# Banded attention with a gated MLP: an own PSUM tile for each MLP accumulator, two attention regions in the first batch, and a new planned order

## The chip, the cores and the metric

The kernel runs on one core of a Trainium2 chip. The metric is device time in microseconds (us), the median of several executions. Lower is better.

## The reference, cut to what matters

```python
# attention: q, k, v are (8 batches, 8 heads, 576 positions, 64)
scores = (q @ k^T) / 8
# heads 0-3: position i sees i-31..i; heads 4-7: every 32nd position up to i
attn = softmax(where(mask, scores, -1e9))          # exp(x - max) / (sum + 1e-9)
x = (attn @ v), heads side by side                  # (8, 576, 512)
# gated MLP: w_in (512, 1024), conv_w (3, 1024), w_out (1024, 512)
h = maximum(x @ w_in, 0)
c = conv_w[0]*h[s-1] + conv_w[1]*h[s] + conv_w[2]*h[s+1]
out = (h * sigmoid(c)) @ w_out
```

The MLP weights come as 64-bit floats.

## The kernel before, in words

**Attention.** Heads go in pairs, four pairs to a batch; a pair is called an attention unit here, numbered n over the whole run. Both masks are turned into a band: the strided heads are permuted so that each of 32 residues is a short local band. For each unit PE computes the scores (36 small matmuls, L459) into a PSUM region `psR[reg]`; VectorE takes the maximum and subtracts it (L470, L471), ScalarE the exponential (L473), VectorE the sum and reciprocal (L474, L476), and GpSimd normalises (L479). The result is transposed into `pt` in one of two ways: *turned* on PE (L439, with ScalarE copies L441), or by 32x32 transposes on VectorE (L482, L502) with ScalarE copies (L499). PE then multiplies by v into the same region (values, L508), and ScalarE and VectorE move it out as a high part `xh` (L522) and a low part `xl` (L523). q, k and v have two buffers (`slot`, n % 2).

**MLP.** Each float32 product is made of three passes over parts of reduced precision: high x high, low x high, high x low. The first product (`mm1`, L545) makes for each of 8 units f of 128 features two groups (halves of 288 positions) of 12 matmuls: four row blocks c times three passes. ScalarE evicts each group with a relu (L551) into one of three `h` buffers; then the convolution: ScalarE scales (L557), VectorE adds two weighted, shifted terms (L563, the "sums"), ScalarE takes the sigmoid (L566), VectorE multiplies (L568, the "gate"), ScalarE rounds to the high part `gh` (L414), and VectorE or GpSimd subtracts for the low part `gl` (L417; SPLIT_G says where). The second product (`mm2`, L585) makes 4 x 2 groups of 24 matmuls, evicted by ScalarE (L591) and written out by DMA (L592).

**Weights.** During the first batch, 8 + 8 weight tiles are loaded as 64-bit words and split into parts by ScalarE and VectorE (`from_f64`), with two matmuls on PE (L393, L394), and, where SPLIT_W says "a", a subtraction of the high part on PE (L400) so that ScalarE can do the last copy (L402) instead of VectorE (L404).

**PSUM.** There are four tiles of 1024 words a partition, r0 to r3. Attention uses the first 576 columns; later batches alternate r0 and r1, and the first batch's four units use r0, r1, r2, r0 (`region`). The four MLP accumulators are halves of r2 and r3:

```python
psR = [psum.tile([P, 1024], F32, name=f"r{i}") for i in range(4)]
psM = [psR[2 + i // 2][:, i % 2 * 512:i % 2 * 512 + 512] for i in range(NPM)]
```

MLP groups take the accumulators in turn (`state["m"] % NPM`), and so do the splits of the second weights; the splits of the first weights use only the two halves of r3.

**Order.** Nothing is written in the order in which it runs. `op` notes each step with an engine, an estimated duration, a due time and the buffers that it reads and writes; there ("M", 0) to ("M", 3) are four separate things. `Plan.order` runs a small model of the engines and emits the steps by their begin times in it. The due times are the table of numbers at the top. Each engine then executes its list strictly in order; the framework that allocates the tiles adds the waits between engines. All loads and stores go through one DMA queue, SP's.

Of the kernel before, what the change touches and what calls it, by code (L numbers as in the profile page):

```python
# [9 lines left out]
F32 = _mybir.dt.float32  # L10
F32R = _mybir.dt.float32r
BF16 = _mybir.dt.bfloat16
I32 = _mybir.dt.int32
# [6 lines left out]
P = 128  # L20
W = 32
# [7 lines left out]
PE_PENALTY = 1  # L29
RATE = 205.0  # L30

EYE_AT = -15.59
CONV_AT = 13.95
FIRST = "w0 k0 q0 v0 k1 w1 q2 q1 v1 k2 c0 w2 w3 q3 k3 v3 v2 w4"
WARM = 4
WARM_SCORES = [0, 0, 2, 4]
WARM_VALUES = [2, 2, 0, 0]
FIRST_AT = [18.9, -9.9, -37.3, -11.6]
SECOND_AT = [45.6, 109.8, 118.7, 107.8]
LATER_AT = [35.8, 46.3, 68.6, 52.7]  # L40
START = 27.38
START2 = 106.92
PERIOD = 46.51
MM1_STEP = 4.82
MM2_AT = 52.57
MM2_STEP = 31.88
LOAD_Q = 76.19
LOAD_V = 12.98
W_IN_AT = [43.1, 1.3, -17.1, 33.6, 22.0, 62.6, 49.8, 27.1]
W_OUT_AT = [55.4, 88.5, 74.3, 73.5, 54.9, 59.3, 84.9, 103.2]  # L50
SPLIT_W = "aavvvaaaaaaaavvv"
SPLIT_G = "vvvpvpvv"
FIRST_SPLIT_G = "vvvvvpvv"
TURNED = 2
FIRST_GATE = "vvvvvvvv"
FIRST_SCALE = "aaaaavaa"


class Plan:
# [184 lines left out]
def tile_banded_attention_gated_mlp(ctx, tc, qT, kT, vw, w_in, conv, w_out, mask, ident, eyes_in, out):  # L244
    nc = tc.nc
    B, NHP, D, _, S = qT.shape
# [7 lines left out]
    V, A, G, T, Q = "dve", "act", "pool", "pe", "dma"  # L254
    plan = Plan()
    op = plan.op
# [32 lines left out]
    cs = [misc[:, c0 + S * i:c0 + S * i + S] for i in range(NHB)]  # L289
    os_ = [misc[:, c0 + S * (NHB + i):c0 + S * (NHB + i) + S] for i in range(2)]  # L290
    psum = ctx.enter_context(tc.tile_pool(name="psum", bufs=1, space=PSUM))
    psR = [psum.tile([P, 1024], F32, name=f"r{i}") for i in range(4)]
    psM = [psR[2 + i // 2][:, i % 2 * 512:i % 2 * 512 + 512] for i in range(NPM)]
    NWS, NWA, NWT, NWL = 3, 2, 2, 1
    words = [const.tile([P, 4 * P, 2], I32, name=f"ws{i}") for i in range(NWS)]
    wa = [const.tile([P, 4 * P], I32, name=f"wa{i}") for i in range(NWA)]
# [5 lines left out]

    def slot(n):
        return n % NB

    def region(n):
        return (0, 1, 2, 0)[n] if n < NHP else n % 2

    def load_q(n, at):
        i, b, hp = slot(n), n // NHP, HPS[n % NHP]  # L310
# [8 lines left out]
    def load_v(n, at):  # L319
        i, b, hp = slot(n), n // NHP, HPS[n % NHP]  # L320
        v = buffers[i][2]
        op(Q, 260, at, lambda: nc.sync.dma_start(out=v, in_=vw[b, hp]), (), [("v", i)])

    def set_up(i, at):
        q, k, v, pt, t = buffers[i][:5]
# [40 lines left out]
    state = dict(m=0, h=0, last=None)  # L366
    seen = set()

    def convert(hi, lo, src, at, key, dat=None):
        c = nw[0]  # L370
        nw[0] += 1
        j, k = c % NWA, c % NWT
        if key[0] == "wi" and c < 3:
            i, ws = ("in", c), misc[:, 1024 * c:1024 * c + 1024].bitcast(I32).rearrange("p (n w) -> p n w", w=2)
        else:
            i, ws = c % NWS, words[c % NWS]
        op(Q, 400, at if dat is None else dat, lambda: nc.sync.dma_start(out=ws.rearrange("p n w -> p (n w)"), in_=src.bitcast(I32)), (), [("W", i)])
        t, tail = wt[k].bitcast(F32), wl[c % NWL]
        kt, kl = ("WT", k), ("WL", c % NWL)
        from_f64(ws[:, :, 1], ws[:, :, 0], wa[j], wt[k], tail, at, ("W", i), ("WA", j), kt, kl, False)  # L380

        def parts(x):
            return x.rearrange("p (c n) -> p c n", c=4)
        if key[0] == "wi":
            mi = 2 + c % 2
        else:
            mi = state["m"] % NPM
            state["m"] += 1
        ps = psM[mi]
# [6 lines left out]
        op(T, 1.1, at, whole, [kt, kl, "unit", "eyer"], [("M", mi)], table=4)  # L396
        if last:
            def rest():
                for x in range(4):
                    nc.tensor.matmul(ps[:, P * x:P * x + P], negr, hi()[:, x, :], start=False, stop=x == 3)  # L400
            op(T, 0.3, at, rest, [(key, "h"), "negr"], [("M", mi)])
            op(A, 0.59, at, lambda: nc.scalar.copy(lo(), parts(ps)), [("M", mi)], [(key, "l")])  # L402
        else:
            op(V, 0.69, at, lambda: nc.vector.tensor_tensor(out=lo(), in0=parts(ps), in1=hi().bitcast(F32), op=ALU.subtract),  # L404
               [("M", mi), (key, "h")], [(key, "l")])
# [25 lines left out]
    def turn(n, ps, ks, u0, n_u, key, at):  # L431
        i = slot(n)
        pt = buffers[i][3]

        def turns():
            for u in range(n_u):
                for e in range(2):
                    o = ps[0:96, 128 * u:128 * u + 128].rearrange("p (h x) -> p h x", h=2)[:, :, 32 * e:32 * e + 32]
                    nc.tensor.matmul(o, pad[:, u0 + u, 32 - 32 * e:128 - 32 * e], unit[:, e, :], start=True, stop=True)  # L439
        op(T, 0.112 * 2 * n_u, at, turns, ["tt", "unit"], [ks], table=3)  # L440
        op(A, 0.25 + 0.105 * n_u, at + 0.5, lambda: nc.scalar.copy(  # L441
            pt[:, :, u0:u0 + n_u, :].rearrange("p h u c -> p u h c"),
            ps[0:96, 0:128 * n_u].rearrange("p (u h c) -> p u h c", h=2, c=64)), [ks], [key])

    def attention(n, at, spread):
        i, hp = slot(n), HPS[n % NHP]
        q, k, v, pt, ta, mx, sm = buffers[i]
        reg = region(n)
        full, ps = psR[reg], psR[reg][:, :S]
        ks = ("M", 2 * reg - 4) if reg > 1 else ("R", reg)  # L450
        ks = [ks, ("M", 2 * reg - 3)] if reg > 1 else [ks, ("R2", reg)]

        def scores():
            for u in range(NU):
# [7 lines left out]
        if n < NHP and WARM_SCORES[n]:  # L462
            def warm_s():
                for _ in range(WARM_SCORES[n]):
# [7 lines left out]
                                                     op=ALU.subtract), ks + [("mx", i)], [("t", i)])  # L472
# [7 lines left out]
                                                     op=ALU.mult), [("t", i), ("sm", i)] + ["zero"] * turned, ["tt" if turned else ("t", i)], lock=True)  # L480
# [224 lines left out]
```

## Time and profile before

| | us |
|---|---|
| median of 3 runs (lowest to highest) | 622.91 (621.85 to 623.96) |
| the profiled execution's own time | 622.13 |
| its span, first to last instruction | 620.2 |
| TensorE (PE) busy | 558.3 (90%) |
| VectorE (DVE) busy | 391.7 (63%) |
| ScalarE (ACT) busy | 342.3 (55%) |
| GpSimd (POOL) busy | 59.0 (10%) |

The mean granted TensorE clock was 0.993 of full speed. In a row of the timeline stand the start, the duration, the engine, the line, the operation, output <- inputs, and in brackets the idle time of the engine before it with what ended that. Buffer numbers are left out there: r is any of r0 to r3. In a row of waits: who waited <- for whom: us in total, times, longest. In a row of groups: busy time, mean ns of one | idle time before. In the chain of waits a count x24 holds the weight load and the matmul where both are seen. A row of windows has the stretch, its length, the busy time of PE, PEld (weight loads), DVE, ACT and POOL, the granted clock, the DMA share and GB/s. "PE busy" counts the latency of matmuls that overlap, so it is not PE at its peak.

### The profile page before, as it was taken

The numbers are of one execution on the slowest core, as the hardware profiler recorded it, in microseconds if no ns is written. First come the engines' busy times: TensorE is split into PE (matmuls) and PEld (weight loads), VectorE is DVE, ScalarE is ACT, GpSimd is POOL, SyncE is SP. The second block draws the span as 40 slices with busy tenths as digits, with TensorE's granted clock in tenths as the row PEclk, the third lists the DMA queues.
The fourth block names the chain that finished last, engine by engine and source line by source line (L and its number), as shares of the span: only waits on it lengthen the run. The fifth ranks groups of instructions, "written<-read, shape, count | busy, mean of one in ns | idle before, by whom it ended". The sixth has DMA issues, their size and how long they took to land.

```text
span 620.2 us, 15601 instructions
## 1 busy us (share of the span) xinstructions
PE 558.3 (90%) x6846; PEld 516.7 (83%) x6846; DVE 391.7 (63%) x622; ACT 342.3 (55%) x639; POOL 59.0 (10%) x66
## 2 busy tenths in 40 slices
PE   2799998999999988989999988999899989998896
PEld 1677886889989988988889988998889888998896
DVE  4568987735878646765776746765776656724630
ACT  2355965645865457445764467446755467435631
POOL 1110100011011100101011100200001101100000
PEclk9799999999999999999999999999999999999999
DMA  8965632126015610443015710452025600100010
GB/s 199 209 202 169 149 102 85 36 87 168 1 31 144 155 49 1 108 133 80 0 40 135 168 37 0 107 153 61 0 72 132 164 11 1 58 32 19 2 39 38
DMA packets 18179, 52.35 MB, mean 84 GB/s; under 512 B 2496, under 2 KB 2688, under 8 KB 18112
## 3 DMA queue, kind: packets, MB, share of 16 engines
q1 hardware_dynamic: 18112, 51.37, 31.5%
q8 instruction: 53, 0.87, 0.6%
q14 instruction: 14, 0.11, 0.1%
HBM read 41.92 MB, written 9.44 MB: 83 GB/s over the span
## 4 chain that ended last, share of the span: by engine, by line
PE 86%; ACT 8%; DMA 3%; issue 2%; DVE 0%; POOL 0%; SPq 0%; ACTq 0%; POOLq 0%
PE r L545 34%; PE r L585 33%; PE r L508 6%; PE r L459 5%; ACT misc L551 4%; PE r L439 3%; PE r L393 2%; DMA q<-in_dram 2%; ACT misc L591 1%; DMA misc<-in_dram 1%; PE r L400 1%; PE r L394 1%; ACT t L473 1%; ACT pt L441 0%; ACT misc L557 0%
## 5 line engine op out<-in xcount | busy, mean ns | idle before, releaser
L545 PE MATMUL r<-xh,wih 128*128 128x288 f32 x512 | 157.2, 307 | 28.9 <-ACT misc L551 27.6
L585 PE MATMUL r<-gh,woh 128*128 128x288 f32 x512 | 156.3, 305 | 9.1 <-ACT misc L591 8.2
L585 PE MATMUL r<-gh,wol 128*128 128x288 f32 x512 | 150.9, 295 | 0.2 <-issue 0.2
L545 PE MATMUL r<-xl,wih 128*128 128x288 f32 x512 | 150.8, 294 | 0.0
L545 PE MATMUL r<-xh,wil 128*128 128x288 f32 x512 | 150.7, 294 | 0.0
L585 PE MATMUL r<-gl,woh 128*128 128x288 f32 x512 | 150.7, 294 | 0.0
L563 DVE SCALAR_TENSOR_TENSOR misc<-misc,cw 128x576 f32<-128x576 f32 x128 | 104.5, 821 | 52.1 <-ACT misc L557 51.0
L545 PEld LDWEIGHTS r<-xh,wih 128*128 128x128 f32 x512 | 96.0, 188 | 43.2 <-ACT misc L551 40.5
L585 PEld LDWEIGHTS r<-gh,woh 128*128 128x128 f32 x512 | 96.0, 187 | 16.2 <-ACT misc L591 12.0
L551 ACT ACTIVATE misc<-r 128x288 f32<-128x288 f32 x128 | 52.5, 412 | 79.9 <-PE r L545 77.3
L585 PEld LDWEIGHTS r<-gh,wol 128*128 128x128 f32 x512 | 96.1, 188 | 0.4 <-issue 0.4
L545 PEld LDWEIGHTS r<-xh,wil 128*128 128x128 f32 x512 | 96.1, 188 | 0.1
L545 PEld LDWEIGHTS r<-xl,wih 128*128 128x128 f32 x512 | 96.1, 188 | 0.0
L585 PEld LDWEIGHTS r<-gl,woh 128*128 128x128 f32 x512 | 96.1, 188 | 0.0
L568 DVE TENSOR_TENSOR misc<-misc 128x576 f32<-128x576 f32 x64 | 51.2, 800 | 34.4 <-ACT misc L566 34.4
L591 ACT COPY misc<-r 128x288 f32<-128x288 f32 x64 | 24.9, 400 | 68.0 <-PE r L585 64.3
L499 ACT COPY pt<-pad 32x288 f32<-32x288 f32 x112 | 48.2, 430 | 16.8 <-DVE pad L482 14.9
L566 ACT ACTIVATE misc<-misc 128x576 f32<-128x576 f32 x64 | 43.8, 685 | 17.3 <-DVE misc L563 16.9
L557 ACT ACTIVATE misc<-misc,cw 128x576 f32<-128x576 f32 x63 | 49.1, 779 | 2.4
L459 PE MATMUL r<-k,q 128*32 128x64 f32 x2304 | 39.1, 225 | 11.6 <-DMA q<-in_dram 8.2
L459 PEld LDWEIGHTS r<-k,q 128*32 128x32 f32 x2304 | 34.9, 113 | 16.1 <-issue 15.5
L479 POOL TENSOR_TENSOR t<-t,sm 128x576 f32<-128x576 f32 x26 | 29.8, 1155 | 192.4 <-DVE sm L476 182.9
(74 smaller groups left out, 603.2 us busy)
## 6 DMA issues: line engine op xcount, KB each, us to landing
v<-in_dram SPq DMA_DIRECT2D x32, 432.0 KB, 3.9
k<-in_dram SPq DMA_DIRECT2D x32, 288.0 KB, 5.7
q<-in_dram SPq DMA_DIRECT2D x32, 288.0 KB, 5.5
out_dram<-misc SPq DMA_DIRECT2D x32, 288.0 KB, 2.1
ws<-in_dram SPq DMA_DIRECT2D x13, 512.0 KB, 3.9
misc<-in_dram SPq DMA_DIRECT2D x3, 512.0 KB, 9.8
k<-in_dram SPq DMA_DIRECT2D x1, 304.0 KB, 8.9
eyes<-in_dram SPq DMA_DIRECT2D x1, 128.0 KB, 9.3
```

The costliest lines, as they stand in the source:

```text
L459: nc.tensor.matmul(ps[j:j + 32, 64 * u:64 * u + 64], q[:, h, W * s:W * s + W], k[:, h, W * s:W * s + 64], start=True, stop=True, tile_posi ...
L479: op(G, 1.152, at + 5.5, lambda: nc.gpsimd.tensor_tensor(out=pn, in0=t, in1=sm.unsqueeze(2).to_broadcast([P, NU, 64]), op=ALU.mult), [("t" ...
L499: op(A, 0.515, at + 7.5, lambda dst=dst, j=j, p=p: nc.scalar.copy(dst, tt[j:j + 32, :, 32 * p:32 * p + 32]), ["tt"], [key])
L508: nc.tensor.matmul(ps[64 * h:64 * h + 64, 64 * u:64 * u + 64], v[:, h, u, :], pt[:, h, u, :], start=True, stop=True, tile_position=(0, 64 ...
L545: nc.tensor.matmul(ps, a[:, c, fs], x[:, c, tok], start=(n == 0 and m == 0), stop=(n == NC - 1 and m == 2))
L551: op(A, 0.405, at + 1.5 * t + 1.7, lambda ps=ps, t=t: nc.scalar.activation(out=h[:, 1 + t * H2:1 + t * H2 + H2], in_=ps, func=AF.Relu), [( ...
L557: op(A, 0.775, at + 3.6, lambda: nc.scalar.activation(out=c_, in_=h[:, 0:S], func=AF.Copy, scale=cw[:, f:f + 1]), kh + ["cw"], [kc] + new)
L563: op(V, 0.811, at + 3.6 + 0.8 * kk, lambda kk=kk: nc.vector.scalar_tensor_tensor(out=c_, in0=h[:, kk:kk + S], scalar=cw[:, kk * NF + f:kk ...
L566: op(A, 0.678, at + 6, lambda: nc.scalar.activation(out=c_, in_=c_, func=AF.Sigmoid), [kc], [kc], table=1)
L568: op(ge, 0.752 if ge == V else 1.43, at + 6.7, lambda: (nc.vector if ge == V else nc.gpsimd).tensor_tensor(out=c_, in0=h[:, 1:S + 1], in1= ...
L585: nc.tensor.matmul(ps, a[:, f, ms], g[:, f, tok], start=(f == 0 and n == 0), stop=(f == NF - 1 and n == 2))
L591: op(A, 0.4, at + 3 * t + 3, lambda ps=ps, tok=tok: nc.scalar.copy(o[:, tok], ps), [("M", mi)], [("o", oi, t)] + (old(c0 + S * (NHB + oi), ...
```

## The change

1. The four MLP accumulators become tiles m0 to m3 of 512 words each; r2 and r3 are gone. PSUM is used to the same size.
2. The first batch's attention units alternate r0 and r1 like all others; `region` is gone.
3. All splits of weights take the four accumulators in turn, with the MLP groups.
4. The subtraction on PE is one matmul of 512 columns instead of four of 128.
5. The planner gets other estimates (loads of v 375 instead of 260, of weights 466 instead of 400, and three on PE) and another table: order of the first loads, due times, and which engine does what. SPLIT_W has 9 "v" instead of 6, SPLIT_G three "p" instead of two, three gates of the first batch go to GpSimd, and one unit of the second batch instead of two is turned on PE (TURNED).

```diff
-FIRST = "w0 k0 q0 v0 k1 w1 q2 q1 v1 k2 c0 w2 w3 q3 k3 v3 v2 w4"
+FIRST = "q0 k0 w0 w1 q1 k1 v0 v1 w3 k2 w2 q3 q2 w4 c0 k3 v3 v2"
...
-SPLIT_W = "aavvvaaaaaaaavvv"
-SPLIT_G = "vvvpvpvv"
-FIRST_SPLIT_G = "vvvvvpvv"
-TURNED = 2
-FIRST_GATE = "vvvvvvvv"
-FIRST_SCALE = "aaaaavaa"
+SPLIT_W = "vvvaaaavvaavvavv"
+SPLIT_G = "vpvvvvpp"
+FIRST_SPLIT_G = "pvvvvvvv"
+TURNED = 1
+FIRST_GATE = "vvvvvppp"
+FIRST_SCALE = "aaaaaaaa"
...
-    psR = [psum.tile([P, 1024], F32, name=f"r{i}") for i in range(4)]
-    psM = [psR[2 + i // 2][:, i % 2 * 512:i % 2 * 512 + 512] for i in range(NPM)]
+    psR = [psum.tile([P, 1024], F32, name=f"r{i}") for i in range(2)]
+    psM = [psum.tile([P, 512], F32, name=f"m{i}") for i in range(NPM)]
...
-    def region(n):
-        return (0, 1, 2, 0)[n] if n < NHP else n % 2
...
-        if key[0] == "wi":
-            mi = 2 + c % 2
-        else:
-            mi = state["m"] % NPM
-            state["m"] += 1
+        mi = state["m"] % NPM
+        state["m"] += 1
...
-                for x in range(4):
-                    nc.tensor.matmul(ps[:, P * x:P * x + P], negr, hi()[:, x, :], start=False, stop=x == 3)
-            op(T, 0.3, at, rest, [(key, "h"), "negr"], [("M", mi)])
+                nc.tensor.matmul(ps, negr, hi(), start=False, stop=True)
+            op(T, 0.23, at, rest, [(key, "h"), "negr"], [("M", mi)])
...
-        reg = region(n)
+        reg = n % 2
         full, ps = psR[reg], psR[reg][:, :S]
-        ks = ("M", 2 * reg - 4) if reg > 1 else ("R", reg)
-        ks = [ks, ("M", 2 * reg - 3)] if reg > 1 else [ks, ("R2", reg)]
+        ks = [("R", reg), ("R2", reg)]
```

Three places in the new order. Line numbers after the change are 8 lower around attention's and the MLP's steps.

PE, from the end of the first group of the third batch's first product, before (xh, xl are the input's parts, wih, wil the weights'; Activation is ScalarE's semaphore):

```order
L545 MATMUL r2_95<-xl_77,wih_78 128x288
L545 MATMUL r2_95<-xh_76,wih_78 128x288
L545 MATMUL r2_95<-xh_76,wil_79 128x288
...
L545 MATMUL r2_95<-xh_76,wih_78 128x288 [waits Activation_49]
...
L545 MATMUL r3_96<-xh_76,wih_78 128x288
```

and after:

```order
L537 MATMUL m0_95<-xl_77,wih_78 128x288
L537 MATMUL m1_96<-xh_76,wih_78 128x288 [waits Activation_49]
L537 MATMUL m1_96<-xh_76,wil_79 128x288
L537 MATMUL m1_96<-xl_77,wih_78 128x288
...
L537 MATMUL m2_97<-xh_76,wih_78 128x288 [waits Activation_49]
```

Before, the second group's first three matmuls have no wait, its fourth waits for ScalarE, and the third group (r3) starts without a wait. Now each group goes into another tile, and the waits stand at groups' starts.

ScalarE in the same product (L551/L543 eviction, L557/L549 scaling, L566/L558 sigmoid, L414/L407 high part), before:

```order
L551 ACTIVATE misc<-r_95 128x288 [waits PE_49] x2
L557 ACTIVATE misc<-misc,cw 128x576 [waits Activation_49,Pool_49]
L551 ACTIVATE misc<-r_96 128x288 [waits PE_49]
L566 ACT_TABLE_LOAD
L566 ACTIVATE misc<-misc 128x576 [waits DVE_49]
```

and after:

```order
L549 ACTIVATE misc<-misc,cw 128x576 [waits Activation_49]
L543 ACTIVATE misc<-m_97 128x288 [waits PE_49]
L558 ACT_TABLE_LOAD
L558 ACTIVATE misc<-misc 128x576 [waits DVE_49]
L543 ACTIVATE misc<-m_98 128x288 [waits PE_49]
L543 ACTIVATE misc<-m_95 128x288 [waits PE_49]
```

Evictions stay between the gates' steps as they did; each one now reads its own tile.

PE at the program's start (k and q make scores, eyes and pad the turning, wt and wl the splits, pt and v the values), before:

```order
L459 MATMUL r_93<-k_59,q_58 32x64 x36
L393 MATMUL r_96<-wt_102,eyes 128x512
L394 MATMUL r_96<-wl_104,eyer 128x512
L400 MATMUL r_96<-wih,negr 128x128 x4
L459 MATMUL r_94<-k_66,q_65 32x64 x36
L439 MATMUL r_93<-eyes,pad 96x2x32 x18
...
L459 MATMUL r_95<-k_59,q_58 32x64 x36
...
L508 MATMUL r_93<-pt_61,v_60 64x64 x18
```

and after:

```order
L451 MATMUL r_93<-k_59,q_58 32x64 x36
L432 MATMUL r_93<-eyes,pad 96x2x32 x8
L451 MATMUL r_94<-k_66,q_65 32x64 x36
L432 MATMUL r_93<-eyes,pad 96x2x32 x10
L387 MATMUL m_95<-wt_104,eyes 128x512
L388 MATMUL m_95<-wl_106,eyer 128x512
...
L500 MATMUL r_93<-pt_61,v_60 64x64 x18
```

The first values (r_93, pt and v) stood behind the third unit's scores (r_95, which is r2); now they stand ahead of them.

SP's queue at the start (misc is the space of the first weights), before:

```order
L607 DMA small<-in_dram 64x128
L377 DMA misc<-in_dram 128x1024
L317 DMA k_59<-in_dram 64x2x576
L312 DMA q_58<-in_dram 64x1152
L322 DMA v_60<-in_dram 96x1152
L331 DMA k_66<-in_dram 64x1216
L317 DMA k_66<-in_dram 64x2x576
L603 DMA eyes<-in_dram 128x256
```

and after:

```order
L599 DMA small<-in_dram 64x128
L309 DMA q_58<-in_dram 64x1152
L314 DMA k_59<-in_dram 64x2x576
L595 DMA eyes<-in_dram 128x256
L374 DMA misc<-in_dram 128x1024 x2
L309 DMA q_65<-in_dram 64x1152
L328 DMA k_66<-in_dram 64x1216
```

The first q and k now come ahead of the first weights (512 KB a tile), and v_60 (432 KB) goes behind the second unit's k.

More of the change, by code (lines that the diff above doesn't have):

```diff
@@ L30 @@
 RATE = 205.0
-EYE_AT = -15.59
-CONV_AT = 13.95
-FIRST = "w0 k0 q0 v0 k1 w1 q2 q1 v1 k2 c0 w2 w3 q3 k3 v3 v2 w4"
+EYE_AT = -18.2
+CONV_AT = 6.62
+FIRST = "q0 k0 w0 w1 q1 k1 v0 v1 w3 k2 w2 q3 q2 w4 c0 k3 v3 v2"
 WARM = 4
@@ L37 @@
 WARM_VALUES = [2, 2, 0, 0]
[L38 to L50, printed above, removed]
-SPLIT_W = "aavvvaaaaaaaavvv"
-SPLIT_G = "vvvpvpvv"
-FIRST_SPLIT_G = "vvvvvpvv"
-TURNED = 2
-FIRST_GATE = "vvvvvvvv"
-FIRST_SCALE = "aaaaavaa"
+FIRST_AT = [0.5, -45.6, -45.5, -7.2]
+SECOND_AT = [19.5, 81.7, 142.9, 125.9]
+LATER_AT = [63.2, 63.2, 97.8, 13.2]
+START = 19.06
+START2 = 92.84
+PERIOD = 46.8
+MM1_STEP = 7.36
+MM2_AT = 58.18
+MM2_STEP = 49.23
+LOAD_Q = 87.67
+LOAD_V = 1.12
+W_IN_AT = [25.6, 9.2, -22.9, 36.0, 19.4, 65.0, 47.3, 0.7]
+W_OUT_AT = [64.0, 75.3, 59.4, 112.2, 29.6, 35.7, 58.1, 94.5]
+SPLIT_W = "vvvaaaavvaavvavv"
[4 more added lines that the diff above has]
+FIRST_SCALE = "aaaaaaaa"
 class Plan:
@@ L321, in load_v @@
         v = buffers[i][2]
-        op(Q, 260, at, lambda: nc.sync.dma_start(out=v, in_=vw[b, hp]), (), [("v", i)])
+        op(Q, 375, at, lambda: nc.sync.dma_start(out=v, in_=vw[b, hp]), (), [("v", i)])
     def set_up(i, at):
@@ L376, in convert @@
             i, ws = c % NWS, words[c % NWS]
-        op(Q, 400, at if dat is None else dat, lambda: nc.sync.dma_start(out=ws.rearrange("p n w -> p (n w)"), in_=src.bitcast(I32)), (), [("W", i)])
+        op(Q, 466, at if dat is None else dat, lambda: nc.sync.dma_start(out=ws.rearrange("p n w -> p (n w)"), in_=src.bitcast(I32)), (), [("W", i)])
         t, tail = wt[k].bitcast(F32), wl[c % NWL]
@@ L395, in convert @@
         op(A, 0.615, at, lambda: nc.scalar.copy(hi(), parts(t)), [kt], [(key, "h")])
-        op(T, 1.1, at, whole, [kt, kl, "unit", "eyer"], [("M", mi)], table=4)
+        op(T, 1.3, at, whole, [kt, kl, "unit", "eyer"], [("M", mi)], table=4)
         if last:
             def rest():
-                for x in range(4):
-                    nc.tensor.matmul(ps[:, P * x:P * x + P], negr, hi()[:, x, :], start=False, stop=x == 3)
-            op(T, 0.3, at, rest, [(key, "h"), "negr"], [("M", mi)])
+                nc.tensor.matmul(ps, negr, hi(), start=False, stop=True)
+            op(T, 0.23, at, rest, [(key, "h"), "negr"], [("M", mi)])
             op(A, 0.59, at, lambda: nc.scalar.copy(lo(), parts(ps)), [("M", mi)], [(key, "l")])
@@ L439, in turns @@
                     nc.tensor.matmul(o, pad[:, u0 + u, 32 - 32 * e:128 - 32 * e], unit[:, e, :], start=True, stop=True)
-        op(T, 0.112 * 2 * n_u, at, turns, ["tt", "unit"], [ks], table=3)
+        op(T, 0.3 * n_u, at, turns, ["tt", "unit"], [ks], table=3)
         op(A, 0.25 + 0.105 * n_u, at + 0.5, lambda: nc.scalar.copy(
```

## Prediction

> **What bounds the kernel now.** I read the page first, then the chain of waits, then the timeline of one steady batch, and the start last. The page:
>
> ```profile
> span 620.2 us, 15601 instructions
> PE 558.3 (90%) x6846; PEld 516.7 (83%) x6846; DVE 391.7 (63%) x622; ACT 342.3 (55%) x639; POOL 59.0 (10%) x66
> ```
>
> TensorE is the bound, with 62 us in which it does nothing; VectorE and ScalarE are far from full. What PE waits for (the list of waits of the whole run, then of its first 149.6 us, then from 557 us on):
>
> ```profile
> PE r L545 <- ACT misc L551: 27.6, 55, 0.5
> PE r L585 <- ACT misc L591: 8.2, 16, 0.5
> ...
> PE r L459 <- DMA q<-in_dram: 8.2, 2, 7.9
> PE r L545 <- ACT misc L551: 2.0, 4, 0.5
> PE r L585 <- ACT misc L591: 0.5, 1, 0.5
> ...
> PE r L545 <- ACT misc L551: 4.0, 8, 0.5
> PE r L585 <- ACT misc L591: 1.6, 3, 0.5
> ```
>
> 71 waits of exactly 0.5 us stand before MLP matmuls, each ended by ScalarE's eviction of an accumulator; 4 + 1 of them are in the first batch, 8 + 3 in the last. Four accumulators should not need that. The timeline of the first product in a steady batch shows what happens:
>
> ```profile
> 285.48 0.30 PE L545 MATMUL r<-xh,wih 128*128 128x288 f32 x1
> ...
> 287.33 0.29 PE L545 MATMUL r<-xl,wih 128*128 128x288 f32 x1
> 287.66 0.41 ACT L551 ACTIVATE misc<-r 128x288 f32<-128x288 f32 x1 [1.58 <-PE r L545]
> 288.13 0.40 PE L545 MATMUL r<-xh,wih 128*128 128x288 f32 x1 [0.50 <-ACT misc L551]
> 288.37 0.29 PE L545 MATMUL r<-xh,wil 128*128 128x288 f32 x1
> 288.50 0.30 PE L545 MATMUL r<-xl,wih 128*128 128x288 f32 x1
> ...
> 291.27 0.29 PE L545 MATMUL r<-xl,wih 128*128 128x288 f32 x1
> 292.07 0.40 PE L545 MATMUL r<-xh,wih 128*128 128x288 f32 x1 [0.50 <-ACT misc L551]
> ```
>
> A group is 12 matmuls. The batch's first product began at 285.48, so 287.33 is its 15th matmul: the eviction of group one starts only when three matmuls of group two are done, and the fourth waits for the eviction's end. Both groups lie in one tile, r2, in two halves that share nothing. So the order of instructions is being kept per tile: the eviction waits for the latest write into the tile, the next write for the eviction. The two products run on at full rate into r3, and there it repeats.
>
> The price of one stop: 21 steps from 288.50 to 291.27 make 0.132 us a matmul; 24 of them would take 3.17, and the two starts after a stop lie 292.07 - 288.13 = 3.94 apart. **0.77 us each**, more than the 0.5 shown, as the pipe also drains and refills.
>
> **The change part by part.** *The stops.* With a tile for each accumulator, a group waits only for the eviction of the group four before it in the cycle, and an eviction only for its own 12 matmuls. 71 x 0.77 = **54.7 us** go, if nothing else is late.
>
> A second way to that sum: a steady batch from its parts.
>
> ```profile
> 149.61 1.99 PE r L545 x15
> ...
> 253.84 0.99 PE r L585 x6
> 254.83 2.15 PE r L459 x144
> ...
> 270.65 2.25 PE r L508 x72
> ...
> 557.02 2.00 PE r L545 x15
> 588.61 12.35 PE r L585 x93
> ```
>
> The lines of the chain at 149.61 and 557.02 are the beginnings of batches 2 and 8: six batches in 407.4 us, 67.9 each. A batch has 384 MLP matmuls (384 x 0.132 = 50.7; the long run at 588.61 has 0.133), two pairs of scores (2 x 2.15), two pairs of values (2 x 2.25) and, by an estimate, 1.2 for six changes between these kinds (0.2 each: six matmuls after a change took 0.99, not 0.79). Together 60.7. The other way: 71 stops less 5 in the first batch and 11 in the last leaves 55, 9.2 a batch, 7.1 us: 67.9 - 7.1 = 60.8. The two agree.
>
> [...] The trace has 132 ns, and that is used.
>
> *Is anything late next?* The rows that decide:
>
> ```profile
> L563 DVE SCALAR_TENSOR_TENSOR misc<-misc,cw 128x576 f32<-128x576 f32 x128 | 104.5, 821 | 52.1 <-ACT misc L557 51.0
> L568 DVE TENSOR_TENSOR misc<-misc 128x576 f32<-128x576 f32 x64 | 51.2, 800 | 34.4 <-ACT misc L566 34.4
> L417 DVE TENSOR_TENSOR gl<-misc,gh 128x576 fp32r<-128x576 f32 x49 | 37.2, 759 | 17.3 <-ACT gh L414 17.2
> L551 ACT ACTIVATE misc<-r 128x288 f32<-128x288 f32 x128 | 52.5, 412 | 79.9 <-PE r L545 77.3
> L557 ACT ACTIVATE misc<-misc,cw 128x576 f32<-128x576 f32 x63 | 49.1, 779 | 2.4
> L566 ACT ACTIVATE misc<-misc 128x576 f32<-128x576 f32 x64 | 43.8, 685 | 17.3 <-DVE misc L563 16.9
> L414 ACT CAST gh<-misc 128x576 fp32r<-128x576 f32 x64 | 42.6, 666 | 8.9 <-DVE misc L568 8.9
> ```
>
> In the first product PE now delivers a unit of 24 matmuls in 3.17 us instead of 3.94. For a unit VectorE has 2 x 0.82 + 0.80 + 0.76 x 5/8 (five of eight low parts, the others on GpSimd) = 2.92 us, ScalarE 2 x 0.41 + 0.78 + 0.69 + 0.67 = 2.96. Both fit, but barely, and ScalarE has a table load and attention's last copies in the same stretch. I walked the new order of a batch through with these durations, from the product's start at 0. Unit 5: evictions end at 18.4 and 19.7, the scaling at 20.5, the two sums at 24.8 (VectorE does the gates of units 3 and 4 in between), the sigmoid at 25.5, the gate at 26.3: 8 us from first eviction to gate, where three buffers of h allow 3 x 3.17 = 9.5. The evictions come 3 to 4 us before the group that needs their tile. PE ends the product at 25.3; it then has 36 matmuls over units 0 to 5 (4.8 us), a pair of values (2.25), 15 matmuls (2.0), a pair of scores (2.15), and wants unit 7 at 36.5. Unit 7: eviction 26.1, scaling 26.9, sums 31.2, sigmoid 31.9, gate 32.7, then two copies of attention ahead of its high part, 33.9, and the low part on GpSimd, 35.2. Cover: 1.3 us, and about the same for unit 6. The later pair of values meets its last copy within 0.3 us. So I charge **0.5 us a batch, 3 us in all**, for new waits. If the cover fails, VectorE's and ScalarE's queues set the pace: bounds 0 to 3 us a batch.
>
> The last batch has no attention to cover its gates, but interleaves four accumulators over units 0 to 6: 4 x 7 x 3 x 0.132 = 11 us against some 8 that the last gate needs. Nothing is charged.
>
> *The start.* The first 149.6 us, by stretches (PE, PEld, VectorE, ScalarE, GpSimd busy, clock, DMA), and the rows that release the first attention units:
>
> ```profile
> 0.00:60.00 60.00, 42.77 (x697) 34.08 (x701) 36.35 (x73) 23.36 (x43) 7.61 (x23) 0.94 0.77 193
> 60.00:113.00 53.00, 48.17 (x474) 41.24 (x464) 43.09 (x73) 39.12 (x70) 4.02 (x3) 1.00 0.40 108
> ...
> 9.85 2.15 PE L459 MATMUL r<-k,q 128*32 128x64 f32 x72 [7.87 <-DMA q<-in_dram]
> 18.00 1.21 PE L459 MATMUL r<-k,q 128*32 128x64 f32 x72 [0.33 <-DMA q<-in_dram]
> 26.25 1.49 PE L459 MATMUL r<-k,q 128*32 128x64 f32 x44 [2.19 <-issue]
> 31.25 1.42 PE L508 MATMUL r<-pt,v 96*64 96x64 f32 x36
> 53.16 1.27 PE L508 MATMUL r<-pt,v 96*64 96x64 f32 x36
> ```
>
> The first scores waited for q0, behind 512 KB of weights; now q0 and k0 go first: at the stretch's mean of 193 GB/s 2.7 us earlier. The second scores get rid of v0's 432 KB ahead of them: 2.2 us. The first values ran at 31.25 because the third scores stood ahead of them in PE's queue and came at 26.25; now the values stand ahead. Against that, the third scores now wait for region 0 to be evicted, where they had r2 to themselves, and their q2 comes later. So the gain shrinks along the chain of heads: between 2 and 11 us at the fourth values (53.16). PE also gets one unit less of turning (2.88 us and more) and single subtracting matmuls instead of four; I count these at nothing, as VectorE is busy 43.1 of 53 us between 60 and 113, and it has the same work as before (more weight splits, fewer gates). What the heads gain must also pass through that stretch. I take **8 us**, bounds -6 to 14: below zero, since the third and fourth heads may come later in the two regions than in three.
>
> *Sum.* The profiled execution took 622.1 (span 620.2 and 1.9 around it): 622.1 - 54.7 - 8 + 3 = 562.4. The median of the runs shown is 0.8 above it: **563 us**.
>
> **The rivals.** *The gates take PE's place* (chance 0.14). Chains on VectorE and ScalarE outlast their cover, at the end of the first product or before a pair of values. For it: 2.92 and 2.96 against 3.17, and cover of 1 us or less. Against it: over the middle six batches VectorE is busy 268 of 407 us, ScalarE 235:
>
> ```profile
> 149.60:557.00 407.40, 378.31 (x4755) 357.63 (x4754) 268.06 (x414) 234.82 (x443) 42.47 (x36) 1.00 0.28 73
> ```
>
> At 2 us more a batch over seven batches: 577.
>
> *The first batch pays* (0.08). Two regions instead of three make the heads serial; 6 us later instead of 8 earlier: 577.
>
> *The stops stay, or as many waits replace them* (0.05). Then only the start gains: 615. That the fence is per tile is inferred; but the halves have nothing else in common, and no stop lies between r2 and r3. [...]
>
> *The clock* (0.03; slower). In the products, PE goes through four accumulators with a hand-over at every group; if its clock were to fall there, matmuls stretch. How much, the start shows: 2.15 us for the scores at 9.85, 1.21 for the same at 18.00 warm, a factor of 1.78. On 50.7 us a batch that is 39.5 times the share of cold time; above a share of 0.18 it eats the 7.1 us, and at a quarter it is 2.8 us a batch too much: 623 - 8 + 7 x 2.8 = 634. Against it stands the clock column, 1.00 from 60 us on with 71 stops in it. [...]
>
> **How the numbers follow.** The forecast has 0.70, and its own range is 551 to 573: 0 to 1.3 us of waits a batch, a start that gains 1 to 14. To hold 8 in 10, I reach into the two cases at 577: **551 to 580**. A difference under about 0.3% (2 us) can't be told from none. Faster: forecast, the first two rivals and most of the third, 0.96; same 0.01; slower 0.03.
>
> **What would show it.** No 0.5 us waits of PE on an eviction in the products; starts of a unit 3.2 us apart; steady batches of 60.7 to 61.5; the second batch's first product at 136 to 142; the first values at about 20. Wrong, if PE waits at a group's start for an eviction or for gl; if batches are 63 or more; if the fourth values come after 53; or if the clock falls below 0.97 after the start.

## The result and the profile after

The changed kernel takes **563.79 us** (median of 4 runs, 563.08 to 564.08) where the kernel before takes 622.38 beside it (4 runs, 619.08 to 623.96): a ratio of 0.9063, with a 95% interval of 0.9025 to 0.9102. The forecast was 563. The profiled execution took 563.75 us. One run in what follows, 582.63 us in experiment 1, is 1.9% above the fastest of its kernel; it counts as slow and is left out of that experiment's median.

The page after, its span and busy times:

```profile
span 561.9 us, 15480 instructions
PE 532.9 (95%) x6777; PEld 509.0 (91%) x6777; DVE 394.0 (70%) x615; ACT 338.7 (60%) x640; POOL 75.5 (13%) x76
```

TensorE's idle time has gone from 62 us to 29. (In the chain of waits a count is of PE's matmuls alone: x192 in 25.44 us is 0.1325 us each. A score or value matmul of the order leaves two records, so that a pair of units has 144 for its scores.) The list of what PE waits for, over the whole run of after (total, times, longest):

```profile
PE r L432 <- POOL pad L471: 6.1, 1, 6.1
PE r L451 <- DMA k<-in_dram: 4.9, 1, 4.9
PE m L577 <- issue: 3.7, 2, 2.3
PE r L451 <- issue: 2.4, 3, 1.5
...
PE r L500 <- DVE pt L494: 1.4, 5, 0.3
```

Not one of the 71 waits for an eviction is left, and none for gl. What a hand-over looks like now, in the timeline of batch 3's first product (L543 is the eviction):

```profile
211.63 0.29 PE L537 MATMUL m<-xh,wil 128*128 128x288 f32 x1
...
211.69 0.41 ACT L543 ACTIVATE misc<-m 128x288 f32<-128x288 f32 x1 [0.62 <-PE m L537]
211.76 0.30 PE L537 MATMUL m<-xl,wih 128*128 128x288 f32 x1
...
211.89 0.29 PE L537 MATMUL m<-xh,wih 128*128 128x288 f32 x1
```

ScalarE reads one accumulator from 211.69 to 212.10 while PE starts a matmul every 0.13 us into another. In the chain of waits the whole first product is therefore one line, where it was broken at every stop before:

```profile
136.17 25.44 PE m L537 x192
...
260.58 25.44 PE m L537 x192
325.51 25.43 PE m L537 x192
...
507.32 25.44 PE m L537 x192
```

These lines give the account. Batch 2 begins at 136.17 instead of 149.61: **13.4 us** from the start. Six batches take 507.32 - 136.17 = 371.2 instead of 407.4, or 61.9 each instead of 67.9: **36.3 us**. From batch 8's beginning to the span's end it is 54.6 instead of 63.2: **8.6 us**. Together 58.3. One of the six is longer than the others, 325.51 - 260.58 = 64.9; experiments 4 and 8 to 12 bear on that.

### The profile page after: what moved, and what is told of

It is laid out like the page before. It is cut to its first block, busy times and chain, and to the rows that moved or that the text cites. A ratio compares the mean times of both kernels' runs of the same rounds, so it can differ in the third digit from the quotient of the medians.

```text
span 561.9 us, 15480 instructions
## 1 busy us (share of the span) xinstructions
PE 532.9 (95%) x6777; PEld 509.0 (91%) x6777; DVE 394.0 (70%) x615; ACT 338.7 (60%) x640; POOL 75.5 (13%) x76
## 4 chain that ended last, share of the span: by engine, by line
PE 81%; DVE 9%; ACT 4%; issue 3%; POOL 1%; DMA 1%; SPq 0%; ACTq 0%; POOLq 0%; DVEq 0%
PE m L537 35%; PE m L577 28%; PE r L451 7%; PE r L500 6%; DVE pt L494 3%; PE r L432 3%; PE m L387 2%; DVE sm L466 1%; DVE pad L474 1%; POOL t L471 1%; DMA k<-in_dram 1%; ACT misc L583 1%; ACT t L465 1%; ACT pt L491 1%; ACT L465 1%
## 5 line engine op out<-in xcount | busy, mean ns | idle before, releaser
L577 PE MATMUL m<-gh,woh 128*128 128x288 f32 x512 | 154.4, 302 | 1.4 <-issue 1.3
L577 PE MATMUL m<-gl,woh 128*128 128x288 f32 x512 | 151.7, 296 | 2.3 <-issue 2.3
L537 PE MATMUL m<-xh,wih 128*128 128x288 f32 x512 | 151.2, 295 | 1.3 <-DVE wol L397 1.2
L577 PE MATMUL m<-gh,wol 128*128 128x288 f32 x512 | 151.4, 296 | 0.0
L537 PE MATMUL m<-xl,wih 128*128 128x288 f32 x512 | 151.1, 295 | 0.0
L537 PE MATMUL m<-xh,wil 128*128 128x288 f32 x512 | 150.8, 295 | 0.0
L577 PEld LDWEIGHTS m<-gh,woh 128*128 128x128 f32 x512 | 96.6, 189 | 4.2 <-issue 1.8
L577 PEld LDWEIGHTS m<-gl,woh 128*128 128x128 f32 x512 | 96.7, 189 | 2.7 <-issue 2.6
L577 PEld LDWEIGHTS m<-gh,wol 128*128 128x128 f32 x512 | 96.7, 189 | 0.0
L537 PEld LDWEIGHTS m<-xh,wil 128*128 128x128 f32 x512 | 96.1, 188 | 0.1
L543 ACT ACTIVATE misc<-m 128x288 f32<-128x288 f32 x128 | 51.7, 406 | 29.5 <-PE m L537 29.2
L549 ACT ACTIVATE misc<-misc,cw 128x576 f32<-128x576 f32 x64 | 49.7, 777 | 2.5
L558 ACT ACTIVATE misc<-misc 128x576 f32<-128x576 f32 x64 | 43.7, 683 | 11.7 <-DVE misc L555 10.2
L407 ACT CAST gh<-misc 128x576 fp32r<-128x576 f32 x64 | 42.6, 667 | 11.0 <-DVE misc L560 7.4
```

The source lines that it names most:

```text
L407: op(A, ta, at, lambda: nc.scalar.copy(hi(), src), [skey], [(key, "h")])
L537: nc.tensor.matmul(ps, a[:, c, fs], x[:, c, tok], start=(n == 0 and m == 0), stop=(n == NC - 1 and m == 2))
L543: op(A, 0.405, at + 1.5 * t + 1.7, lambda ps=ps, t=t: nc.scalar.activation(out=h[:, 1 + t * H2:1 + t * H2 + H2], in_=ps, func=AF.Relu), [( ...
L549: op(A, 0.775, at + 3.6, lambda: nc.scalar.activation(out=c_, in_=h[:, 0:S], func=AF.Copy, scale=cw[:, f:f + 1]), kh + ["cw"], [kc] + new)
L558: op(A, 0.678, at + 6, lambda: nc.scalar.activation(out=c_, in_=c_, func=AF.Sigmoid), [kc], [kc], table=1)
L577: nc.tensor.matmul(ps, a[:, f, ms], g[:, f, tok], start=(f == 0 and n == 0), stop=(f == NF - 1 and n == 2))
```

## Experiments

Two theories first. **T**: the order of instructions is kept per tile, so that two accumulators in one tile stop PE at each hand-over; a tile for each takes the stops away, and the plan gives only the start. **P**, the rival: the new plan's order does most of it, and the tiles matter little. The pauses that the list calls "issue" came up in the profile after; theories on them (**F**: loads that run at that moment; **I**: the place in PE's stream of instructions) stand with experiments 8 to 12.

### 1. The tiles without the plan

The kernel before, with the two edits that give the accumulators tiles of their own:

```diff
-    psR = [psum.tile([P, 1024], F32, name=f"r{i}") for i in range(4)]
-    psM = [psR[2 + i // 2][:, i % 2 * 512:i % 2 * 512 + 512] for i in range(NPM)]
+    psR = [psum.tile([P, 1024], F32, name=f"r{i}") for i in range(2)]
+    psM = [psum.tile([P, 512], F32, name=f"m{i}") for i in range(NPM)]
...
-        return (0, 1, 2, 0)[n] if n < NHP else n % 2
+        return n % 2
```

> The kernel before with its whole old table, but with an own tile for each accumulator and the two attention regions. Theory T (the stops are a fence per tile): 622 - 54.7 = 568, and up to 6 more for the heads that become serial in two regions: 566 to 576, with no 0.5 us waits of PE on an eviction. Theory P (the gain comes from the new order): 610 or more.

Measured: 574.86 us (3 runs, 571.52 to 579.89), ratio 0.9265 (0.9199 to 0.9332). The chain:

```profile
149.75 25.43 PE m L545 x192
...
518.16 25.44 PE m L545 x192
```

Six batches take 368.4 us, 61.4 each, with no wait for an eviction: the steady gain is there without the new plan. The start gains nothing, 149.75 against 149.61, although its 5 stops are gone too. Two regions instead of three, in an order planned for three, would explain that, but it is not shown: TensorE's granted clock was also at half for 17.1 us of this start (37.1 to 43.9 and 54.2 to 64.4), for 6.8 us of the start before (24.8 to 31.6) and, in the clock's records, which begin at 20.4 us there, never in that of after. So the plan's part is 574.86 - 563.79 = 11.1 us by the medians, give or take the 4 us by which the runs of this experiment differ. In the profiles it is all in the start, 149.75 - 136.17 = 13.6; the six steady batches are even 2.8 us shorter here than in after, which fits the pauses in them (2.6 us here, 5.4 in after).

### 2. The plan without the tiles

The changed kernel, with the accumulators put back in pairs into r2 and r3; every engine's instructions stand in the order of the changed kernel:

```diff
-    psR = [psum.tile([P, 1024], F32, name=f"r{i}") for i in range(2)]
-    psM = [psum.tile([P, 512], F32, name=f"m{i}") for i in range(NPM)]
+    psR = [psum.tile([P, 1024], F32, name=f"r{i}") for i in range(4)]
+    psM = [psR[2 + i // 2][:, i % 2 * 512:i % 2 * 512 + 512] for i in range(NPM)]
```

> The changed kernel with the accumulators put back as halves of two tiles; every engine's list of instructions is the same as after the change. T: the stops come back, 71 of 0.77 us if as many as before, 564 + 55 = 618 (600 to 625, since groups now alternate more often between the halves of a tile in the second product). P: 564 to 567.

Measured: 618.43 us (10 runs, 616.54 to 621.62), ratio 0.9952 (0.993 to 0.9973). What PE waits for:

```profile
PE r L537 <- ACT misc L543: 26.4, 52, 0.6
PE r L577 <- ACT misc L583: 10.8, 21, 0.5
```

Two lines of the chain, where batches 2 and 8 begin:

```profile
141.36 1.98 PE r L537 x15
...
551.89 2.00 PE r L537 x15
```

The same instructions in the same order, and the shared tiles alone bring 73 stops back: 618.43 - 563.79 = 54.6 us, 0.75 each; 68.4 us a batch. P falls.

### 3. Half of the tiles

The kernel before with only the second pair split. Its order is untouched, so that only the fence in r3 goes:

```diff
-    psR = [psum.tile([P, 1024], F32, name=f"r{i}") for i in range(4)]
-    psM = [psR[2 + i // 2][:, i % 2 * 512:i % 2 * 512 + 512] for i in range(NPM)]
+    psR = [psum.tile([P, 1024], F32, name=f"r{i}") for i in range(3)]
+    psM = [psR[2][:, i * 512:i * 512 + 512] for i in range(2)]
+    psM += [psum.tile([P, 512], F32, name=f"m{i}") for i in (2, 3)]
```

> The kernel before with only r3 split into two tiles, r2 still shared; every engine's list is the same as before. T: about half of the stops go, 622 - 27 = 595 (588 to 602), and the waits that are left stand before groups in r2 alone. P: 622. Theory M (the stop only moves to the next hand-over, since PE is held by something else): 612 or more.

Measured: 587.19 us (4 runs, 585.98 to 592.83), ratio 0.9468 (0.9424 to 0.9512). What PE waits for:

```profile
PE r L546 <- ACT misc L552: 13.1, 26, 0.5
PE r L586 <- ACT misc L592: 1.1, 2, 0.5
```

And the chain of waits through a part of batch 7's first product:

```profile
474.88 3.18 PE m L546 x24
478.06 2.39 PE r L546 x18
...
480.47 0.42 ACT misc L552
...
480.93 1.06 PE r L546 x6
481.99 3.18 PE m L546 x24
```

Read the last five lines as a pair: 24 matmuls into the tiles of their own run through, 24 into the shared tile stop for an eviction, in one and the same product. The time is just under the 588 that was expected at least, as the gain is larger than half: 28 stops are left, all in r2, so 43 of the 71 went; 621.25 (before, beside this run) - 587.19 = 34.1 us, 0.79 each. The stops that went did not turn up at the next hand-over, so theory M falls too.

### 4. Four subtractions again

The changed kernel with the four small matmuls of the weights' split (L393) instead of one, which the prediction counted at nothing:

```diff
-                nc.tensor.matmul(ps, negr, hi(), start=False, stop=True)
+                for x in range(4):
+                    nc.tensor.matmul(ps[:, P * x:P * x + P], negr, hi()[:, x, :], start=False, stop=x == 3)
```

> The changed kernel with the subtraction on PE as four matmuls of 128 columns again, same order. As predicted (hidden behind VectorE, counted at nothing): 563.8, within 1 us. If it is part of what the start gained beyond the forecast: seven times 0.5 us, 567.

Measured: 561.47 us (6 runs, 559.47 to 564.03), ratio 0.904 (0.9011 to 0.9069), an interval that overlaps with that of after: no cost. It is below both times that were expected; from the first, 563.8, it can't be told apart. What did move are the pauses: with more matmuls in the first batch they lie elsewhere in the steady ones, and are 3.1 us in all instead of 6.1.

### 5. Two units turned again

```diff
-TURNED = 1
+TURNED = 2
```

> The changed kernel with two units of the second batch turned on PE instead of one, planned anew. If PE's time in the rest of the first batch is what the start lives on: 3 us more (2.9 to 3.5 of turning), 567. As in the prediction (hidden behind VectorE): 563.8, within 1.5 us.

Measured: 568.71 us (5 runs, 567.21 to 568.98), ratio 0.9148 (0.9119 to 0.9177); the changed kernel run beside it took 563.53 (ratio 0.9067, 0.9037 to 0.9097). **5.2 us**, where the prediction had nothing. Two lines of its chain, the second product of the first batch and the first of the second:

```profile
105.68 8.33 PE m L577 x63
...
140.40 25.44 PE m L537 x192
```

In after they begin at 100.70 and 136.17. The delay, 5.0 and then 4.2 us, is there from the second product on (3.1 at the second place against the profile of experiment 7, where it is 137.34). The order was planned anew here and in experiment 6, so each shows what its setting is worth with the plan that follows from it.

### 6. The old order of the first loads

```diff
-FIRST = "q0 k0 w0 w1 q1 k1 v0 v1 w3 k2 w2 q3 q2 w4 c0 k3 v3 v2"
+FIRST = "w0 k0 q0 v0 k1 w1 q2 q1 v1 k2 c0 w2 w3 q3 k3 v3 v2 w4"
```

> The changed kernel with the old order of the first loads (FIRST of the kernel before), planned anew. If the loads' order is what lets the heads start early: the first scores come at 9.9 instead of 6.9 and the first product of the second batch 3 to 8 us later, 567 to 572. If it is hidden by what follows: 563.5, within 1.5 us.

Measured: 572.88 us (4 runs, 571.49 to 578.23), ratio 0.9228 (0.9186 to 0.9269): 9.3 us slower than the changed kernel's 563.53 (experiment 7), a little above the 567 to 572 that was expected. Its first scores in the timeline:

```profile
9.92 2.15 PE L451 MATMUL r<-k,q 128*32 128x64 f32 x72 [7.94 <-DMA q<-in_dram]
```

What VectorE waits for most in the first 140 us:

```profile
DVE wa L344 <- ACT wa L343: 11.8, 8, 2.7
```

The stretch from its fourth values on, in the columns of the prediction's stretches:

```profile
53.50:100.00 46.50, 40.13 (x365) 31.97 (x366) 34.15 (x60) 29.27 (x54) 3.24 (x3) 0.89 0.47 134
```

The scores come 3.0 us later than in after and the fourth values 3.9 (53.49 against 49.57), yet the second product begins 10.4 us later (111.13 against 100.70). In between VectorE is busy for only 34.15 of 46.5 us, as it waits for the first steps of the weights' splits on ScalarE; PE idles with it, and its granted clock is 0.89 in this stretch, at half for 10.2 us. How much of that is weights that come late is open: from 49 to 105 us ScalarE's own waits for them are 2.5 us here and 1.0 in after.

### 7. The changed kernel again

> The changed kernel once more, on the chip of the next three, to compare them with: 563.8, within 2 us.

Measured: 563.53 us (4 runs, 562.53 to 564.62), the same as after. Its pauses lie at the same places, 2.9 + 2.8 us in all.

### 8 and 9. Smaller, and later, loads of q and k

What are the pauses? The chain of after through the long batch, where PE stops between two matmuls of the second product:

```profile
312.54 2.15 PE r L451 x144
314.68 0.87 PE m L577 x5
315.55 2.33 issue
317.88 7.63 PE m L577 x46
```

The timeline there:

```profile
315.25 0.30 PE L577 MATMUL m<-gh,wol 128*128 128x288 f32 x1
317.88 0.61 PE L577 MATMUL m<-gl,woh 128*128 128x288 f32 x1 [2.33 <-issue]
...
318.52 0.44 PE L577 MATMUL m<-gh,wol 128*128 128x288 f32 x1
318.76 0.44 PE L577 MATMUL m<-gl,woh 128*128 128x288 f32 x1
```

Three stretches around it, with granted clock, DMA share and GB/s as the last three columns:

```profile
311.00:317.00 6.00, 4.55 (x173) 3.99 (x168) 4.70 (x7) 1.98 (x5) 0.00 (x0) 1.00 0.91 218
315.00:320.00 5.00, 2.67 (x14) 2.43 (x13) 3.69 (x8) 1.66 (x3) 1.47 (x2) 0.73 1.02 211
320.00:325.00 5.00, 5.00 (x37) 5.00 (x37) 3.32 (x7) 2.01 (x5) 0.80 (x1) 0.93 0.36 94
```

Nothing that the trace records releases PE after 2.33 us. It comes soon after 144 short score matmuls in 2.15 us, while the DMA engines are full (1.02 of their time, 211 GB/s) with the later units' v, q and k. Then the granted clock is 0.73 over 5 us and matmuls start 0.24 us apart instead of 0.13. From the scores' end (314.69) to the next first product it takes 10.8 us instead of the 7.0 of the batch before: 3.9 us for one pause.

Experiment 8 shrinks the q and k loads of the units from the fourth batch on from 576 columns to 32 (`qT[b, hp][:, :, 0:W] if n >= 12 else ...`, k alike). Experiment 9 keeps them whole and holds those of the last units of a batch back until the next product has begun:

```diff
+                if f == 0:
+                    begun = [state["last"]]
...
-                    load_q(n, at - LOAD_Q)
-                    load_k(n, at - LOAD_Q)
+                    later = begun if b and j >= 2 else ()
+                    load_q(n, at - LOAD_Q, later)
+                    load_k(n, at - LOAD_Q, later)
```

> The changed kernel, but from the fourth batch on each load of q and k moves only the first 32 of 576 columns (so the output is not the reference's there); all other instructions and their order are the same. Theory F (PE's pauses without a named releaser, 0.3 to 2.3 us after the scores, come while q and k loads fill the DMA engines, and PE's own instructions come over the same engines): the pauses go from the third batch on and every steady batch takes 60.7 to 61.2 us, 3 to 6 us less in all: 558 to 561. Theory I (the pauses are PE's own, from the many short score matmuls): the pauses stay, 563 to 565.

> The changed kernel, but the q and k loads of each batch's last two attention units, which are needed some 40 us later, stand behind the batch's last two stores in the DMA queue, so they start in the next first product instead of right after the scores; every other engine's list is unchanged. F: the pauses after the second pair of scores go, 1 to 2 us in the batches that had them, 558 to 562, faster than the changed kernel. I: the same as the changed kernel, within 1 us.

Measured: 563.28 us (6 runs, 559.65 to 565.19; ratio 0.9054, 0.9022 to 0.9086) and 561.50 us (5 runs, 560.43 to 563.53; ratio 0.9036, 0.9008 to 0.9064). Neither can be told from after, though experiment 9 lies in the 558 to 562 that theory F expected. Experiment 8 still pauses 2.3 + 1.9 us, 9 still 2.1 + 3.3, its longest 2.4 in the same place as after's. Theory F as stated, that q's and k's loads do it, is not borne out. But the loads of v, issued just ahead, ran on in both.

### 10. Twenty instructions more

The changed kernel with ten more warming matmuls (20 PE instructions) at the very start, which nothing later depends on:

```diff
-        for _ in range(WARM):
+        for _ in range(WARM + 10):
```

> The changed kernel with ten more warming matmuls at the very start (20 instructions on PE, in time in which it waits for the first load), nothing else. If PE's pauses hang on where its instructions lie in its stream (theory I): the pauses come at other places, with other lengths, and the time moves by 1 to 4 us either way. If they hang on the loads (theory F): the same places, 563.5, within 1 us.

Measured: 564.09 us (6 runs, 563.24 to 567.62), ratio 0.9079 (0.9052 to 0.9107). The pauses of PE between 130 and 520 us (in after 2.4 us before scores, none above 1.5, and 3.7 in the second product):

```profile
PE r L451 <- issue: 5.9, 4, 3.1
```

Now all of them stand before score matmuls, the longest inside the scores at 313.5 instead of behind them. So 20 more instructions ahead of them were enough to move the pauses. The sum is about the same (5.9 against 6.1), and the time did not move by the 1 to 4 us that theory I expected.

### 11 and 12. All later loads out of the way

Experiment 11 is experiment 8 with v's later loads cut too, to 1 of 64 columns (`v[:, :, 0:1] if n >= 12 else v`): hardly any load is left in the later batches. Experiment 12 computes everything: it is experiment 9 with the first two units' v held back in the same way:

```diff
-                    load_v(n, at - LOAD_V)
+                    load_v(n, at - LOAD_V, begun if b and j < 2 else ())
```

> The changed kernel, but from the fourth batch on loads of q and k move 32 of 576 columns and loads of v one of 64 (output not the reference's there); order unchanged. F: without traffic the pauses after the third batch go, 557 to 560. I: they stay at the same places, shorter or not, 561 to 564.

> The changed kernel with all loads that follow the second half of each second product (v, then q and k, needed 25 us or more later) behind the batch's last two stores in the DMA queue, so that they run in the next first product; the other engines' lists are unchanged. Theory FI (a pause needs both: a place in PE's stream where its next instructions are due, and loads that fill the DMA engines then): the pauses after the later scores go, those after the earlier scores (0.3 to 0.6 us) stay, 559 to 561.5, against 563.5 for the changed kernel and 557.3 without later loads. If the place alone decides: 563.5, within 1 us.

Measured: 557.28 us (6 runs, 556.53 to 559.72; ratio 0.8956, 0.893 to 0.8983) and **557.99 us** (6 runs, 557.11 to 559.15; ratio 0.8979, 0.8956 to 0.9002). Experiment 12 is faster than the 559 to 561.5 that was expected. Experiment 11's profile has 0.9 us of pauses between 130 and 520 us. Those of experiment 12:

```profile
PE r L451 <- issue: 1.0, 2, 0.8
PE m L577 <- issue: 0.7, 2, 0.5
```

The stretch that had the longest pause:

```profile
311.00:317.00 6.00, 5.76 (x170) 5.43 (x170) 5.11 (x9) 1.66 (x3) 0.00 (x0) 1.00 0.15 53
```

Batches 2 and 8 in its chain:

```profile
136.42 25.44 PE m L537 x192
...
501.64 25.44 PE m L537 x192
```

With the loads moved to where PE runs long matmuls, the pauses shrink to a quarter (1.7 us), PE is busy 5.76 of 6 us where it was 4.55, and a batch takes 60.9 us. Experiment 12 beats both kernels: 5.5 us under the changed one (563.53), with intervals of the ratio well apart. So in these runs the longest pauses came with both, a burst of short matmuls at a certain place in PE's stream and DMA engines that are full with loads (a share of 0.91 from 311 to 317 us in after, 0.15 here).

The kept traces show what that place is. Count PE's records (matmuls, weight loads, its sequencer's) in order of start: in all 14 traces together there are 51 pauses of "issue" over 0.2 us, and every one comes after 193 or 194 records more than a multiple of 256. After's longest comes after 8130 = 31 x 256 + 194; in experiment 10 it comes after 8130 too, so that the 20 more instructions put another matmul there. One of the DMA queues is listed as carrying instructions, in packets of 16 KB in the trace of after; its line of that page (packets, MB, share):

```profile
q8 instruction: 53, 0.87, 0.7%
```

These are 53 packets for 13,620 records, which make 53.2 times 256. Each of the 51 pauses ends 1.2 to 1.7 us after the packet of its number (the 31st for the multiple 31) has landed. In after PE began the block of 256 records ahead of the longest pause at 312.77 us, and the 31st packet ran from 315.30 to 316.52; in experiment 12 PE began that block at 311.27, the packet ran from 311.52 to 312.97, and the pause is 0.24 us. In the burst a block lasts about 3 us, in the long products 17. The packet began 2.5 us after that block's beginning in after, with a DMA share of 1.12 in between, and 0.25 us after it in experiment 12, where the share is 0.15 from 311 to 317 us. My reading is that PE paused because it was through with a block before the next one had come, and that the full DMA engines made the next one late. That, and that the packets are PE's own, is inferred from these counts and times; no run moved the packets alone.

## Why the prediction was right

The mechanism was right, and the stops are most of the change. That the sum came within 1 us is in part luck: the steady batches gave 36.3 us where 39.4 were forecast (55 x 0.77 less 3), and the start gave 13.4 where 11.9 were.

**The stops: right.** 71 x 0.77 was the main term. Experiment 2 gives 0.75 a stop and experiment 3 gives 0.79, with nothing else changed on any engine. That the fence goes by tile was inferred; experiment 3 shows it within one product, and experiment 2 with the new order. In experiment 1, with a tile to each accumulator, PE runs 192 matmuls in 25.43 us through the evictions.

**Steady batches: right, but the pauses were missing.** Forecast 60.8 + 0.5, measured 61.9. The later pair of values waits its 0.3 us, as walked through; no wait of PE for gl is in its list, so the gates' cover held in every batch, and their rival did not come. The 0.6 us a batch beyond the forecast are the pauses, which it did not have, though a row that it quoted, the third scores of before at 26.25 with 2.19 of "issue", has one of that kind. With most of them gone (experiment 12) a batch takes 60.9. The one batch of 64.9, above the 63 that the prediction called a sign of being wrong, is the one with the longest pause. The sum from parts, 60.7, was 0.4 too high for a mean of these six: the last of them has one pair of scores and not two (58.7 us in after).

**The start: right in sum, wrong inside.** Forecast 8 + 5 x 0.77 = 11.9, measured 13.4. Scores and values of the first units in after:

```profile
6.93 2.15 PE L451 MATMUL r<-k,q 128*32 128x64 f32 x72 [4.95 <-DMA k<-in_dram]
15.20 2.82 PE L432 MATMUL r<-eyes,pad 128*96 128x64 f32 x16 [6.12 <-POOL pad L471]
17.95 2.15 PE L451 MATMUL r<-k,q 128*32 128x64 f32 x72
...
23.77 1.27 PE L500 MATMUL r<-pt,v 96*64 96x64 f32 x36
...
49.57 1.27 PE L500 MATMUL r<-pt,v 96*64 96x64 f32 x36
```

The first scores gain 2.9 (forecast 2.7). The second gain nothing (forecast 2.2): they stand in PE's queue behind the first unit's turning (L432), and that waits 6.1 us for GpSimd. This wait takes the place of the one for q's load, which had stood behind v0's; the order after showed it, and I did not read it. The first values come at 23.8, where I had about 20, and the fourth gain 3.6, within the bounds of 2 to 11, but well under the 8 that I took for the start. That term was mis-sized. Even those 3.6 need not all be the order's: before, the granted clock was at half from 24.8 to 31.6 us, from inside the pause of 2.19 on, and in after it was not; no run parts the two. The missing part came from behind it:

```profile
52.40:99.00 46.60, 44.90 (x399) 36.94 (x397) 44.38 (x77) 36.24 (x68) 4.19 (x3) 1.00 0.50 141
```

The first batch's second product begins, by the chains of before and after, at:

```profile
113.14 1.61 PE r L585 x12
...
100.70 8.46 PE m L577 x63
```

From the fourth values to it, it is 100.70 - 49.57 = 51.1 us; before, 113.14 - 53.16 = 60.0. That is 8.9 us, and four of the five stops, 3.1 us, are in it; the rest of the first batch gives 1.0, with the fifth. VectorE, busy 81% of the time from 60 to 113 us before (43.1 of 53), now has 95%. So "VectorE is busy and has the same work" was the failing step: it still had 10 us of holes there. The order of the first loads does much to close them (experiment 6, where it is undone: 9.3 us, and the holes are back); by which step is not shown. "One unit less of turning counts at nothing" failed as well: 5.2 us (experiment 5). "Single subtracting matmuls count at nothing" held (experiment 4). Undone one at a time, these parts give more than 13.4 together with the stops; they overlap. What two regions cost by themselves is open (experiment 1).

**The last batch: right.** 8.6 for 11 x 0.77 = 8.5; nothing was charged for its gates, and none waits.

**The clock: did not fall at the hand-overs.** It fell once after the start, to half for 3.4 us from 317.3 us on, beginning inside the longest pause, and the whole batch around that has 0.97. The batch from 387.6 on has a granted clock of 1.00 through all its hand-overs:

```profile
387.60:448.60 61.00, 60.71 (x818) 59.63 (x817) 45.40 (x70) 39.02 (x75) 8.77 (x7) 1.00 0.35 90
```

## What to carry to other kernels

If an engine waits half a microsecond at regular places, and the wait stands in the middle of a group rather than at its start, ask which two things share a tile, not which engine is slow; put each accumulator that is handed over by itself into a tile of its own, and price the stop by the distance of starts with and without it (0.77 us here), not by the wait shown (0.5). An engine that is 80% busy in a stretch need not be the bound there (VectorE here: 81% before, 95% after): list what its holes wait for before counting a change ahead of it at nothing. Try bulk loads where the matrix engine runs long matmuls instead of beside its bursts of short ones (5.5 us here). If an engine pauses without a releaser, count its records up to each pause: a common remainder (193 or 194 of 256 here), with packets of an instruction queue that land shortly (1.2 to 1.7 us here) ahead of each pause's end, suggests the coming of its instructions.

## What the runs showed of the hardware

- PE paused with no recorded releaser, 0.2 to 3.1 us at a time, behind or within bursts of short matmuls: 6.1 us in all from 130 to 520 us in after, 1.7 us with the loads moved. The longest of after, 2.33 us, came with the DMA engines at 1.02 of their time and 211 GB/s (315 to 320 us). All 51 such pauses in the 14 traces come after 193 or 194 PE records more than a multiple of 256, and end 1.2 to 1.7 us after the 16 KB packet of the same number in an instruction queue.
- In that pause, when PE had been idle for 1.8 us, the granted clock fell to half for 3.4 us (from 317.3 on; 0.73 over the 5 us around it). Behind it matmuls were 0.24 us apart instead of 0.13, and from the scores' end to the next first product it took 3.9 us more than in the batch before.
